# Loads of the last tokens' values without a common key, and small transfers of a recurrent step fewer and spread out

## The chip, the cores and the metric

The kernel runs on one core of one Trainium2 chip. Time is the device time in microseconds (us) of one execution, given as the median of several.

The names used below are PE (TensorE, matmul), ACT (ScalarE), DVE (VectorE), POOL (GpSimd) and SP (SyncE; here it computes nothing and only issues DMAs). "SPq" is SP's sequencer. "ring" is a set of SBUF buffers through which weights are streamed.

## The reference, cut to what matters

Two branches are mixed by a gate. Branch A is recurrent: 64 segments of 32 tokens, each with 8 memory rows in front of it. The first 8 output rows of a segment are the memory of the next.

```python
for s in range(n_seg):                               # 64 segments
    xs = x[:, s * seg_len:(s + 1) * seg_len, :]
    h = jnp.concatenate([mem, xs], axis=1)           # 8 + 32 rows of 1024
    q, k, v = (jnp.einsum('btd,dhe->bhte', h, W) for W in (Wq, Wk, Wv))   # shortened; 32 heads of 128
    ...                                              # masked softmax attention
    o = jnp.einsum('bhte,hed->btd', o, Wo)
    mem = o[:, :M, :]
    outs.append(o[:, M:, :])
b = gelu(x @ w_gate) * (x @ w_up) @ w_down           # branch B, an FFN, 1024 to 3584 to 1024
return g * a + (1 - g) * b
```

Wq, Wk, Wv and Wo are 8 MB each in bf16, 32 MB together, and every segment needs all of them. SBUF holds only a part, so the rest is read from HBM again in each of the 64 steps.

## The kernel before: the parts that matter

The weights are 64 pieces of 512 KB. 43 stay in SBUF. 21 are streamed in every step through a ring of five buffers. SP issues all transfers of a step in program order. The q, k, v of the last 8 tokens of a segment ("rest") don't depend on the memory, so they are computed once at the start and loaded in small parts (`vB`, `qkr`). The memory rows attend to these tokens too, so a step needs them; but their own output is not needed for the next memory, and its projection is done after the loop.

A helper records every operation with the regions that it reads and writes, and works out the waits. The line to keep in mind is the one for writes: a DMA that writes a region waits for the region's last writer.

```python
def _touch(self, op, reg, write, async_):
    # ... (cut) a region is a set of SBUF cells, or a key such as ("D", "v", 3)
    for k in keys:
        w, rd = c                                  # last writer, readers since
        if write:
            if w is not None and (w.sem is not None or w.eng != op.eng or async_):
                deps.append(w)                     # a DMA waits for the writer before it
            # ... and for the readers

def load_str():                                    # the next streamed piece, into the ring
    n = nst[0]; nst[0] += 1
    p, t = seq[n], ring[n % NRING]
    op("sp", lambda e: e.dma_start(dst(t, p), src(p)), wr=[t.r()], lane=f"ring{n % NRING}")

def load_v(s):                                     # values of the last 8 tokens: 4 groups x 8 partitions
    for g in range(4):
        op("sp", lambda e, g=g: e.dma_start(vB[32 * g:32 * g + 8, :, :]..., v_scr[g, NB * s:NB * s + NB, :]),
           rd=[("D", "v", NB * s // RB)], wr=[vB.r()], lane=f"vb{g}")

def start_step():                                  # runs at piece 2 of a step
    put_rest(s)                                    # four POOL copies out of qkr
    for f in pend: f()                             # the stores of the step before
    pend.clear()
    if not last:
        load_h(s + 1)
        load_qk(s + 1)

on(55, lambda: attend(1))                          # the last reader of vB in a step
on(56, lambda: load_v(s + 1) if not last else None)
for p in range(64):
    for f in at.get(p, ()): f()
    proj(p, s)                                     # matmuls of piece p; then load_str() if p is streamed

def store(s=s):
    for g in range(4):
        op("sp", lambda e, g=g: e.dma_start(a_scr[s, 0:NR, g * 256:(g + 1) * 256], a_bf[32 * g:32 * g + NR, :]), ...)
    op("sp", lambda e: e.dma_start(o_scr[:, s, :], orr...), ...)
pend.append(store)

def load_a(T):                                     # in the FFN: branch A's result for 128 tokens
    op("sp", lambda e: e.dma_start(asb[T % 2][:, :], a_scr[4 * T:4 * T + 4].rearrange("s t f -> (s t) f")), ...)
```

## Time and profile before

| | before |
|---|---|
| median time | 3469.65 us |
| a recurrent step | 39.0 us, 64 of them |
| DMA share, rate in the loop | 0.84, 294 GB/s |
| PE clock granted in the loop | 0.81 |
| FFN, from its first matmul to the end | 613.1 us |

The length of a step is the distance of the DVE writes of the next memory into `hT`: the first starts at 316.6 us, the 63rd at 2735.4 us, and there are 62 steps between them.

The page shows the span in 40 equal slices, one digit each, in tenths. PE and DMA are busy shares, PEclk is the granted PE clock.

```profile
span 3479.6 us, 84141 instructions
PE   6685666776677676777667667776776679999998
PEclk9897787888788877877878887888788889999999
DMA  7658878887888888888888888888888761514414
```

Slices 4 to 31, counted from 0, are the loop. Neither PE nor the DMA engines are full there. That calls for a closer look at one step. The windows view gives, for a stretch of time, the busy time of each engine, then the PE clock, the mean share of the 16 DMA engines and their rate. The share is the summed time of the packets over the time of 16 engines; it can pass 1, because packet records of one engine can overlap. The first line is the loop, the others are one step's end.

```profile
core 0: us, PE busy (x) PEld busy (x) DVE busy (x) ACT busy (x) POOL busy (x), PEclk, DMA share, GB/s
316.60:2735.40 2418.80, 1692.67 (x33604) 694.31 (x33604) 406.07 (x1303) 427.29 (x1116) 97.53 (x310) 0.81 0.84 294
...
1093.00:1095.00 2.00, 1.70 (x56) 1.21 (x52) 0.56 (x2) 0.50 (x2) 1.19 (x4) 1.00 1.08 405
1097.00:1099.00 2.00, 1.72 (x18) 0.69 (x22) 0.19 (x1) 0.00 (x0) 0.00 (x0) 0.66 0.17 62
1099.00:1101.50 2.50, 2.33 (x24) 0.68 (x16) 0.00 (x0) 0.41 (x1) 0.00 (x0) 0.59 0.05 13
1101.50:1106.00 4.50, 0.64 (x8) 0.29 (x12) 0.00 (x0) 0.19 (x1) 0.00 (x0) 0.83 0.67 214
```

The DMA engines go from full to almost nothing at 1097 us. PE still has some pieces then, and after 1101.5 us it has hardly any (0.64 us busy of 4.5). The timeline of SP in order of time tells why (start, length, line, destination and source, count).

```profile
1092.63 0.34 SPq L340 DMA_DIRECT2D ring_80<-in_A_Wk_dram  x1
1093.02 8.80 SPq L554 DMA_DIRECT2D vB<-v_scr  x4
1101.86 0.36 SPq L340 DMA_DIRECT2D ring_81<-in_A_Wq_dram  x1
...
1103.21 1.74 SPq L788 DMA_DIRECT2D a_scr<-a_bf  x4
1104.99 0.35 SPq L790 DMA_DIRECT2D o_scr<-orr  x1
1105.38 0.43 SPq L545 DMA_DIRECT2D hT_55<-xq_scr  x1
1105.86 0.46 SPq L549 DMA_DIRECT2D qkr<-qk_scr  x1
1106.36 0.50 SPq L340 DMA_DIRECT2D ring_79<-in_A_Wk_dram  x1
```

The four vB loads take 8.80 us of SP. The waits view (engine, line, what it waited for: us in total, times, longest) shows what it was waiting for over the whole loop.

```profile
SPq L340 <- PE pb L701: 868.0, 683, 4.4
SPq L554 <- DMA vB<-v_scr: 472.1, 189, 7.3
```

The first line is harmless in itself: SP waits until PE has freed a ring buffer. The second is a wait of one DMA for another; 189 is three waits in each of 63 steps.

### The profile page before, as it was taken

Reading aid. Unit: us, or ns where it says so; the run is one execution under the profiler, and the core shown is the slowest. Engines: PE = TensorE matmul, PEld = TensorE weight load, DVE = VectorE, ACT = ScalarE, POOL = GpSimd, SP = SyncE. Lnnn points to the kernel's source line nnn. Section 1 sums busy time; section 2 is a strip of 40 time slices with the busy share of each in tenths; the row PEclk is TensorE's granted clock in tenths of the full one; section 3 lists DMA queues with packets and bytes.
Section 4 is the critical chain, followed back from the end, with each engine's and each line's share of the span. In section 5 each row is a group of like instructions: output and inputs, shape, how many; then the busy total and the mean of one; then the engine's idle time right before and its main releaser. Section 6 shows DMA issues by size and latency. Waiting matters only on the chain.

```text
span 3479.6 us, 84141 instructions
## 1 busy us (share of the span) xinstructions
PE 2584.2 (74%) x38522; PEld 1095.3 (31%) x38566; DVE 758.9 (22%) x1837; ACT 631.1 (18%) x1453; POOL 143.5 (4%) x383
## 2 busy tenths in 40 slices
PE   6685666776677676777667667776776679999998
PEld 3332222332223222223222222232222234444443
DVE  1311111111111111111111111111111106344353
ACT  1111111111112111111111111111111113122121
POOL 2200000000000000000000000000000000000000
PEclk9897787888788877877878887888788889999999
DMA  7658878887888888888888888888888761514414
GB/s 238 181 140 297 288 277 296 305 307 268 292 301 306 286 290 294 296 292 278 290 297 296 293 283 300 301 312 282 302 290 311 278 237 52 206 66 140 151 61 151
DMA packets 440962, 881.35 MB, mean 253 GB/s; under 512 B 131736, under 2 KB 166552, under 8 KB 440096
## 3 DMA queue, kind: packets, MB, share of 16 engines
q1 hardware_dynamic: 362960, 849.49, 69.5%
q10 hardware_dynamic: 77648, 26.48, 3.2%
q8 instruction: 302, 4.95, 0.6%
q14 instruction: 52, 0.43, 0.0%
HBM read 846.48 MB, written 29.36 MB: 252 GB/s over the span
## 4 chain that ended last, share of the span: by engine, by line
DMA 47%; PE 42%; SPq 6%; issue 3%; DVE 2%; ACTq 1%; ACT 0%
PE pb L701 13%; DMA vB<-v_scr 12%; PE pb L919 11%; PE pb L953 4%; PE pb L712 3%; DMA ring_82<-in_A_Wk_dram 3%; PE pb L486 3%; DMA ring_82<-in_A_Wo_dram 2%; DMA ring_79<-in_A_Wo_dram 2%; DMA ring_80<-in_A_Wo_dram 2%; DMA ring_80<-in_A_Wk_dram 2%; DMA ring_78<-in_A_Wo_dram 2%; SPq L788 2%; DMA ring_81<-in_A_Wo_dram 2%; DMA ring_79<-in_A_Wk_dram 2%
## 5 line engine op out<-in xcount | busy, mean ns | idle before, releaser
L568 ACT ACTIVATE tok_76<-pb 128x512 bf16<-128x512 f32 x128 | 76.4, 597 | 615.1 <-PE pb L701 615.1
L568 ACT ACTIVATE tok_77<-pb 128x512 bf16<-128x512 f32 (+1 forms) x128 | 62.8, 490 | 545.9 <-PE pb L701 545.9
L571 DVE COPY kT_69<-pb 128x512 bf16<-128x512 bf16 x64 | 27.2, 424 | 574.3 <-PE pb L585 574.3
L927 ACT ACTIVATE s_162<-pb 128x512 f32<-128x512 f32 x112 | 66.8, 596 | 326.9 <-DVE osb_164 L968 172.5
L770 POOL COPY orr<-oT 128x256 bf16<-128x256 bf16 x64 | 25.6, 400 | 2383.0 <-DVE oT L571 2383.0
L571 DVE COPY qT_65<-pb 128x512 bf16<-128x512 bf16 x64 | 27.2, 424 | 438.2 <-PE pb L585 438.2
L571 DVE CAST oT<-pb 128x160 bf16<-128x160 f32 x256 | 71.1, 319 | 217.2 <-PE pb L682 217.2
L568 ACT ACTIVATE oT<-pb 128x160 bf16<-128x160 f32 x256 | 63.8, 301 | 248.6 <-PE pb L682 248.6
L701 PE MATMUL pb<-ring_78,hT_56 128*32 128x512 bf16 x384 | 47.7, 486 | 62.1 <-DMA ring_78<-in_A_Wq_dram 43.1
L701 PE MATMUL pb<-ring_78,hT_55 128*32 128x512 bf16 x384 | 47.1, 479 | 59.5 <-DMA ring_78<-in_A_Wk_dram 30.5
L701 PE MATMUL pb<-ring_82,hT_56 128*32 128x512 bf16 x384 | 46.9, 477 | 57.3 <-DMA ring_82<-in_A_Wq_dram 37.4
L701 PE MATMUL pb<-ring_81,hT_56 128*32 128x512 bf16 x384 | 45.2, 459 | 59.0 <-DMA ring_81<-in_A_Wq_dram 40.2
L701 PE MATMUL pb<-ring_79,hT_56 128*32 128x512 bf16 x384 | 46.8, 475 | 53.9 <-DMA ring_79<-in_A_Wq_dram 34.3
L701 PE MATMUL pb<-ring_80,hT_56 128*32 128x512 bf16 x384 | 45.5, 462 | 55.2 <-DMA ring_80<-in_A_Wq_dram 35.1
L701 PE MATMUL pb<-ring_80,hT_55 128*32 128x512 bf16 x384 | 47.6, 484 | 47.4 <-DMA ring_80<-in_A_Wq_dram 25.6
L701 PE MATMUL pb<-ring_82,hT_55 128*32 128x512 bf16 x384 | 47.4, 482 | 44.3 <-DMA ring_82<-in_A_Wq_dram 23.8
L701 PE MATMUL pb<-ring_81,hT_55 128*32 128x512 bf16 x384 | 47.4, 481 | 43.1 <-DMA ring_81<-in_A_Wq_dram 26.0
L701 PE MATMUL pb<-ring_79,hT_55 128*32 128x512 bf16 x384 | 47.4, 482 | 42.4 <-DMA ring_79<-in_A_Wq_dram 25.6
L611 DVE TENSOR_REDUCE nm_58<-pb 128x8 f32<-128x320 f32 x64 | 31.5, 492 | 197.6 <-PE pb L607 197.6
L953 PE MATMUL pb<-wd_141,GT 128*128 128x512 bf16 x299 | 70.0, 386 | 5.3 <-DMA wd_141<-in_B_w_down_dram 5.0
L953 PE MATMUL pb<-wd_140,GT 128*128 128x512 bf16 x294 | 67.9, 379 | 3.0 <-DMA wd_140<-in_B_w_down_dram 2.4
L568 ACT ACTIVATE kT_70<-pb 128x512 bf16<-128x512 bf16 x64 | 38.2, 597 | 175.3 <-PE pb L585 175.3
(482 smaller groups left out, 5186.5 us busy)
## 6 DMA issues: line engine op xcount, KB each, us to landing
ring_82<-in_A_Wq_dram SPq DMA_DIRECT2D x80, 512.0 KB, 7.2
ring_80<-in_A_Wq_dram SPq DMA_DIRECT2D x78, 512.0 KB, 7.2
ring_81<-in_A_Wq_dram SPq DMA_DIRECT2D x78, 512.0 KB, 7.4
ring_78<-in_A_Wo_dram SPq DMA_DIRECT2D x78, 512.0 KB, 6.8
ring_79<-in_A_Wo_dram SPq DMA_DIRECT2D x78, 512.0 KB, 6.7
ring_80<-in_A_Wo_dram SPq DMA_DIRECT2D x78, 512.0 KB, 6.6
ring_81<-in_A_Wo_dram SPq DMA_DIRECT2D x78, 512.0 KB, 6.7
ring_78<-in_A_Wq_dram SPq DMA_DIRECT2D x78, 512.0 KB, 7.2
```

What stands on the lines that cost most here:

```text
L486: ins = e.matmul(PB[b][:, 0:NRT], lhsT=w8[kc][:, c:c + 128], rhs=xrT[:, kc, :], start=(kc == 0), stop=(kc == KC - 1))
L568: op("act", lambda e: e.activation(o, i, ACTF.Copy), rd=rd, wr=wr)
L571: op("dve", lambda e: e.tensor_copy(o, i), rd=rd, wr=wr)
L611: op("dve", lambda e: e.tensor_reduce(nm[u][:, :, :].rearrange("p a b -> p (a b)"), PB[SS][:, 0:320].rearrange("p (a c) -> p a c", c=LQ), ...
L701: ins = e.matmul(PB[bk][32 * g:32 * g + 32, :], lhsT=h[:, kc, :], rhs=w[:, g * 512:(g + 1) * 512], start=(kc == 0), stop=(kc == KC - 1))
L712: ins = e.matmul(PB[A0][32 * g:32 * g + 32, 0:256], lhsT=oT[:, u, gp, 2 * jj + hh, 0:32], rhs=w[:, c:c + 256], start=(p == 48 and hh == 0) ...
L770: op("pool", lambda e: e.tensor_copy(orr[:, :, :, :].rearrange("p u x c -> p (u x) c"), oT[:, :, :, :, 32:40].rearrange("p u g j c -> p (u ...
L788: op("sp", lambda e, g=g: e.dma_start(a_scr[s, 0:NR, g * 256:(g + 1) * 256], a_bf[32 * g:32 * g + NR, :]), rd=[a_bf.r()], wr=[("D", "a", s ...
L919: ins = e.matmul(PB[bk][:, 0:FB], lhsT=w[:, kc, cc:cc + 128], rhs=xT[:, :, :, kc, :].rearrange("p t i c -> p (t i) c"), start=(kc == 0), s ...
L927: op("act", lambda e, hg=hg: e.activation(s1[:, :], hg, ACTF.Square, scale=SQ), rd=[BK(bg)], wr=[s1.r()])
L953: ins = e.matmul(PB[bank[2 * k + hf]][:, :], lhsT=GT[:, j, tb * 128:(tb + 1) * 128], rhs=w[:, jj, hf * 512:(hf + 1) * 512], start=(j == 0) ...
```

## The change

It has three parts. (1) Each vB group gets its own key, so that the four loads no longer wait for each other. (2) The four stores of `a_bf` become one, into a raw layout; the price is that the FFN has to collect a block of 128 tokens by eight DMAs instead of one. (3) The loads of h and qk for the next step move from piece 2 to pieces 5 and 8. The diff, cut to its core (the FFN's small buffers are also placed by a new allocator, which is cut here):

```diff
+        op("pool", lambda e: e.memset(nm[0][:, 0:1, 0:1], 0.0), rd=[vB.r()], wr=[("D", "vB", g) for g in range(4)])
 ...
-                   rd=[("D", "v", NB * s // RB)], wr=[vB.r()], lane=f"vb{g}")
+                   rd=[("D", "v", NB * s // RB)], wr=[("D", "vB", g)], lane=f"vb{g}")
 ...
-            op("pe", f, rd=[vA[u].r(), vB.r(), EE[u].r()], wr=[BK(b) for b in bo])
+            op("pe", f, rd=[vA[u].r(), EE[u].r()] + [("D", "vB", g) for g in range(4)], wr=[BK(b) for b in bo])
 ...
-                if not last:
-                    load_h(s + 1)
-                    load_qk(s + 1)
             on(2, start_step)
+            on(5, lambda: load_h(s + 1) if not last else None)
+            on(8, lambda: load_qk(s + 1) if not last else None)
 ...
-                for g in range(4):
-                    op("sp", lambda e, g=g: e.dma_start(a_scr[s, 0:NR, g * 256:(g + 1) * 256], a_bf[32 * g:32 * g + NR, :]),
-                       rd=[a_bf.r()], wr=[("D", "a", s // 4, "m", s, g)], lane=f"st{g}")
+                op("sp", lambda e: e.dma_start(a_raw[s, :, :], a_bf[:, :]), rd=[a_bf.r()], wr=[("D", "a", s)], lane="st")
 ...
-            op("sp", lambda e: e.dma_start(asb[T % 2][:, :], a_scr[4 * T:4 * T + 4].rearrange("s t f -> (s t) f")), ...)
+            for i in range(4):
+                for key, lo, hi, ap in (("m", 0, NR, a_raw[4 * T + i].rearrange("(g r) c -> r g c", g=4)[0:NR]),
+                                        ("r", NR, SEG, a_rest[32 * T + 8 * i:32 * T + 8 * i + 8].rearrange("r (g c) -> r g c", g=4))):
+                    op("sp", lambda e, lo=lo, hi=hi, ap=ap, i=i: e.dma_start(
+                        t[32 * i + lo:32 * i + hi, :].rearrange("r (g c) -> r g c", g=4), ap), ...)
```

More of the change, by code (lines that the diff above doesn't have):

```diff
@@ L246, in bass_gated_mix__memory_aug_recurrent_mem_tr__geglu_ffn__prompt_kernel @@
         o_scr = nc.dram_tensor("o_scr", [128, NSEG, 256], BF16)
-        a_scr = nc.dram_tensor("a_scr", [NSEG, SEG, D], BF16)
+        a_raw = nc.dram_tensor("a_raw", [NSEG, 128, 256], BF16)
+        a_rest = nc.dram_tensor("a_rest", [NRT, D], BF16)
         PB = [es.enter_context(nc.psum_tensor(f"pb{i}", [128, 512], FP32)) for i in range(8)]
@@ L814, in bass_gated_mix__memory_aug_recurrent_mem_tr__geglu_ffn__prompt_kernel, with al2 @@
         orT = [orT0, al("orT1", [128, SB, 256], at=low)]
-        cur[0] = low + 8192
         arb = [al(f"arb{i}", [128, D], at=wd[0].off + 4096 + 2048 * i) for i in range(2)]
         orX = [al("orX0", [128, 32, SB, NB], at=wg[3].off), al("orX1", [128, 32, SB, NB], at=wd[1].off)]
-        asb = [al(f"asb{t}", [128, D]) for t in range(2)]
-        tp = [al(f"tp{t}", [128, FB], FP32) for t in range(2)]
-        s1 = al("s1", [128, FB], FP32)
-        osb = [al(f"osb{t}", [128, D]) for t in range(2)]
-        dsb = [al(f"dsb{t}", [128, 512], FP32) for t in range(2)]
-        assert cur[0] <= res0
+        free = [(low + 8192, res0), (cur[0], top), (0, low if ring[0].off < low else 0)]
+        def al2(name, shape, dt=BF16):
+            nb = shape[1] * (4 if dt == FP32 else 2)
+            for k, (lo, hi) in enumerate(free):
+                if lo + nb <= min(hi, 16384 if lo < 16384 else hi):
+                    free[k] = (lo + nb, hi)
+                    return al(name, shape, dt, at=lo)
+            raise AssertionError(name)
+        asb = [al2(f"asb{t}", [128, D]) for t in range(2)]
+        tp = [al2(f"tp{t}", [128, FB], FP32) for t in range(2)]
+        s1 = al2("s1", [128, FB], FP32)
+        osb = [al2(f"osb{t}", [128, D]) for t in range(2)]
+        dsb = [al2(f"dsb{t}", [128, 512], FP32) for t in range(2)]
         def load_or(b):
@@ L893, in bass_gated_mix__memory_aug_recurrent_mem_tr__geglu_ffn__prompt_kernel @@
             dve_copy(ab[0:RB, 512:1024], PB[bs[1]][0:RB, :], [BK(bs[1])], [ab.r(512, 1024)])
-            op("act", lambda e, b=b, ab=ab: e.dma_start(a_scr[SB * b:SB * b + SB, NR:SEG, :],
-                                                       ab[0:RB, :]),
+            op("act", lambda e, b=b, ab=ab: e.dma_start(a_rest[RB * b:RB * b + RB, :], ab[0:RB, :]),
                rd=[ab.r()], wr=[("D", "ar", T) for T in range(SB * b // 4, (SB * b + SB) // 4)], lane=f"ar{b % 2}")
@@ L906, in load_a @@
         def load_a(T):
-            op("sp", lambda e: e.dma_start(asb[T % 2][:, :], a_scr[4 * T:4 * T + 4].rearrange("s t f -> (s t) f")),
-               rd=[("D", "a", T, "m", s, g) for s in range(4 * T, 4 * T + 4) for g in range(4)] + [("D", "ar", T)],
-               wr=[asb[T % 2].r()], lane=f"al{T % 2}")
+            t = asb[T % 2]
+            for i in range(4):
+                for key, lo, hi, ap in (("m", 0, NR, a_raw[4 * T + i].rearrange("(g r) c -> r g c", g=4)[0:NR]),
+                                        ("r", NR, SEG, a_rest[32 * T + 8 * i:32 * T + 8 * i + 8].rearrange("r (g c) -> r g c", g=4))):
+                    op("sp", lambda e, lo=lo, hi=hi, ap=ap, i=i: e.dma_start(
+                        t[32 * i + lo:32 * i + hi, :].rearrange("r (g c) -> r g c", g=4), ap),
+                       rd=[("D", "a", 4 * T + i) if key == "m" else ("D", "ar", T)], wr=[("D", "asb", T % 2, i, key)],
+                       lane=f"al{T % 2}{i}{key}")
         for fb in range(NFB):
@@ L966, in bass_gated_mix__memory_aug_recurrent_mem_tr__geglu_ffn__prompt_kernel @@
                             out=d[:, :], in0=asb[T % 2][:, cs], in1=PB[b][:, :], op=ALU.subtract),
-                           rd=[BK(b), asb[T % 2].r()], wr=[d.r()])
+                           rd=[BK(b)] + [("D", "asb", T % 2, i, k) for i in range(4) for k in "mr"], wr=[d.r()])
                         op("dve", lambda e, T=T, b=b, cs=cs, ob=ob, d=d: e.scalar_tensor_tensor(
```

## The prediction

> **What bounds it now.** The program has a start (to about 265 us), 64 recurrent steps (to about 2776 us), a pass over the last tokens, and the FFN. A step takes 39.0 us (distance of the DVE writes into hT). In the windows view the loop keeps the DMA engines 0.84 busy at 294 GB/s and PE about 0.70: neither is full. A step streams 21 weight pieces of 512 KB through 5 ring buffers, issued by SP in program order. The waits view for SP shows the hole: L554 (values of the last tokens, vB) waits for earlier vB loads, 472 us in total. All four write one recorded region, so each waits for the one before: first about 5.5 us (it queues behind ring pieces), then 1.5 and 1.5 us with nothing else queued. Behind them come three ring loads, four stores of a_bf (1.7 us of issue), o, h and qk. At 1097 to 1101.5 us the DMA share is 0.17 and 0.05. About 6.5 us of DMA time a step is idle, nearly all there. PE runs dry about 9.2 us a step on ring DMAs, and its clock after the gap is 0.5 to 0.6.
>
> **What changes.** (1) One key per vB group: four issues, about 1.1 us of SP, no wait; ring loads follow. (2) One a_bf store for four: 1.3 us less issue, 16 KB more. (3) The h and qk loads move three and six pieces later; qk waits for four POOL copies of 0.29 us, which at its old place would now stall SP. (4) Cost: an asb load becomes 8 DMAs of 512 B rows; SP issues 16 instead of 2 ahead of the w_down loads, twice per FFN block.
>
> **How much is critical.** Steps: packets add up to 32.8 us per step of 16 engines (about 29 at their median durations), the new floor. PE's own chain is 39.0 - 9.2 = 29.8 us, part of it at half clock, and should shorten. Both are close, so overlap won't be perfect: 33.0 us a step, an estimate. Gain 6.0 x 63.5 = 380 us.
> FFN: 14 more issues at 0.23 to 0.4 us, 3 to 5 us per pair. w_down is issued right after asb (2993.05, then 2993.43 us), and its landing (6.7 us) already ends a PE wait in the chain. I expect 3 us at each of 8 places, 25 us lost. The rest stays.
>
> 3470 - 380 + 25, about **3115 us**, range 3030 to 3220. Faster by over 2%: 0.97; within 2%: 0.02; slower: 0.01.
>
> The Trainium skill agrees on two points: "DMA: Bandwidth & Descriptors", Rules for kernel authors, says transfers under 64 KB pay mostly overhead (here a lone 16 KB vB load takes 1.5 us); "TensorE: Matmul & The Clock Gate", Part 1, says idling halves the clock (here 0.5 to 0.6 after the gap).
>
> **What would show it.** Steps of 32 to 34 us; SP's wait on vB gone from the waits, vB gone from the chain; DMA share in the loop 0.95 or more at about 340 GB/s; no slices near 0.05 at a step's end; loop clock up from 0.81; SP waiting for PE (L701, L712) to free ring buffers. In the FFN: longer PE waits on w_down, about 25 us in all.
>
> **What would make it wrong.** Five buffers too few to carry DMA over the step's end, so that DMA idles waiting for PE: 34 to 35 us a step. Packets that stretch when the queue is always full: share rises, GB/s doesn't. Or the reverse: median packets and a warmer PE give 30 to 31 us, about 3000. The FFN loss could be larger if 512 B rows on few engines block the w_down loads behind them.

## The result, and the profile after

| | before | after |
|---|---|---|
| median time | 3469.65 us | 2994.8 us |
| ratio, 95% interval | | 0.8637 [0.8606, 0.8668] |
| a recurrent step | 39.01 us | 31.18 us |
| DMA share, rate in the loop | 0.84, 294 GB/s | 1.01, 368 GB/s |
| PE clock in the loop | 0.81 | 0.95 |
| FFN | 613.1 us | 632.8 us |

A ratio here is the mean time of one kernel's runs over the mean of the other's of the same rounds, so it is not quite the ratio of the medians. Executions over 1.5% slower than the fastest of the same kernel are left out of the means.

The change is faster by 13.6%. The direction and the mechanism were predicted. The time was not: 2994.8 us lies below the range of 3030 to 3220 us.

The page of the changed kernel, the same lines as before:

```profile
span 2990.3 us, 84293 instructions
PE   5687777777777777777777777787776999989998
PEclk9888999999999999999999999899998999999999
DMA  8666999999999999999999999999999415060705
```

In the loop the DMA digits are now all 9, and the PE clock is 9 in all of its slices but one. The windows view of the loop and of one step's end:

```profile
310.40:2243.60 1933.20, 1485.29 (x33604) 650.19 (x33604) 405.86 (x1303) 429.68 (x1116) 97.51 (x310) 0.95 1.01 368
...
1023.00:1025.00 2.00, 1.86 (x77) 1.16 (x74) 0.56 (x2) 0.50 (x2) 0.62 (x2) 1.00 1.05 397
1025.00:1027.00 2.00, 1.35 (x36) 0.71 (x32) 0.00 (x0) 0.00 (x0) 0.95 (x4) 1.00 1.05 387
1027.00:1029.00 2.00, 1.06 (x18) 0.55 (x22) 0.48 (x2) 0.28 (x1) 0.00 (x0) 1.00 1.00 316
```

And the timeline of SP over the same place of a step:

```profile
1023.31 0.34 SPq L341 DMA_DIRECT2D ring_78<-in_A_Wk_dram  x1
1023.70 1.34 SPq L556 DMA_DIRECT2D vB<-v_scr  x4
1025.08 0.36 SPq L341 DMA_DIRECT2D ring_79<-in_A_Wq_dram  x1
...
1027.63 0.33 SPq L788 DMA_DIRECT2D a_raw<-a_bf  x1
1028.00 0.43 SPq L789 DMA_DIRECT2D o_scr<-orr  x1
1029.32 0.33 SPq L341 DMA_DIRECT2D ring_82<-in_A_Wk_dram  x1
1029.70 0.43 SPq L547 DMA_DIRECT2D hT_56<-xq_scr  x1
1030.17 0.47 SPq L341 DMA_DIRECT2D ring_78<-in_A_Wk_dram  x1
1030.69 0.55 SPq L551 DMA_DIRECT2D qkr<-qk_scr  x1
```

The vB loads take 1.34 us instead of 8.80 us, the wait on vB is gone from the waits view, and the small transfers stand between ring loads instead of in one block.

Where the 489.3 us between the two profiled spans (3479.6 and 2990.3 us) come from: 62 steps at 7.83 us each are 485.6 us; the start is 6.2 us shorter; from the last write of `hT` to the FFN it is 17.2 us shorter (131.1 to 113.9 us; the last step lies in it); the FFN is 19.7 us longer.

The prediction had a step fall to 33.0 us, because the packets of a step summed to 32.8 us of 16 engines, and it called that sum the new floor. The step went below it. The sum itself fell: 0.84 x 39.01 is 32.8 us, and 1.01 x 31.18 is 31.5 us. By the packet records of the trace between the first and the last write of `hT`, the mean packet of 4096 bytes (pieces of Wq, Wk, Wv) took 184.8 ns before and 174.3 ns after, with the same number of them and a median of 159 ns in both. So the question for the experiments was: what had stretched the packets before, and which part of the change took it away?

### The profile page after: what moved, and what is told of

Read it like the earlier page. It is cut to its first block, busy times and chain, and to the rows that moved or that the text cites. A ratio compares the mean times of both kernels' runs of the same rounds, so it can differ in the third digit from the quotient of the medians.

```text
span 2990.3 us, 84293 instructions
## 1 busy us (share of the span) xinstructions
PE 2381.1 (80%) x38566; PEld 1052.3 (35%) x38566; DVE 758.7 (25%) x1837; ACT 633.6 (21%) x1453; POOL 143.6 (5%) x384
## 4 chain that ended last, share of the span: by engine, by line
DMA 50%; PE 42%; issue 3%; SPq 2%; DVE 2%; ACT 1%; ACTq 1%; DVEq 0%
PE pb L929 12%; PE pb L703 9%; DMA ring_78<-in_A_Wq_dram 5%; DMA ring_81<-in_A_Wq_dram 5%; DMA ring_82<-in_A_Wq_dram 5%; PE pb L963 4%; DMA ring_79<-in_A_Wq_dram 4%; PE pb L714 4%; DMA ring_80<-in_A_Wq_dram 4%; DMA ring_80<-in_A_Wo_dram 3%; PE pb L488 3%; DMA ring_82<-in_A_Wo_dram 3%; DMA ring_81<-in_A_Wo_dram 3%; DMA ring_80<-in_A_Wv_dram 2%; DMA ring_78<-in_A_Wo_dram 2%
## 5 line engine op out<-in xcount | busy, mean ns | idle before, releaser
L963 PE MATMUL pb<-wd_141,GT 128*128 128x512 bf16 x304 | 73.2, 397 | 7.8 <-DMA wd_141<-in_B_w_down_dram 7.8
L573 DVE CAST a_bf<-pb 128x128 bf16<-128x128 f32 x64 | 18.6, 291 | 233.6 <-ACT a_bf L570 233.6
L963 PE MATMUL pb<-wd_140,GT 128*128 128x512 bf16 x304 | 71.9, 392 | 5.4 <-DMA wd_140<-in_B_w_down_dram 5.4
L963 PE MATMUL pb<-wd_142,GT 128*128 128x512 bf16 x288 | 69.6, 398 | 6.1 <-DMA wd_142<-in_B_w_down_dram 6.1
L703 PE MATMUL pb<-ring_78,hT_55 128*32 128x512 bf16 x384 | 42.0, 417 | 39.7 <-DMA ring_78<-in_A_Wk_dram 17.2
L703 PE MATMUL pb<-ring_81,hT_56 128*32 128x512 bf16 x384 | 40.3, 406 | 31.9 <-DMA ring_81<-in_A_Wq_dram 16.3
L570 ACT ACTIVATE a_bf<-pb 128x128 bf16<-128x128 f32 x64 | 17.7, 277 | 217.5 <-PE pb L714 217.5
L929 PE MATMUL pb<-xT,wg_144 128*128 128x512 bf16 x224 | 56.2, 396 | 7.9 <-DVE GT L945 7.9
L703 PE MATMUL pb<-ring_82,hT_56 128*32 128x512 bf16 x384 | 39.6, 397 | 27.6 <-DMA ring_82<-in_A_Wq_dram 13.9
L703 PE MATMUL pb<-ring_82,hT_55 128*32 128x512 bf16 x384 | 40.0, 403 | 25.9 <-DMA ring_82<-in_A_Wq_dram 15.4
L573 DVE CAST tok_77<-pb 128x256 bf16<-128x256 f32 x64 | 27.1, 424 | 131.8 <-ACT tok_77 L570 131.8
L703 PE MATMUL pb<-ring_80,hT_55 128*32 128x512 bf16 x384 | 39.9, 401 | 25.7 <-DMA ring_80<-in_A_Wk_dram 12.3
```

The lines of the kernel that those rows point to most:

```text
L570: op("act", lambda e: e.activation(o, i, ACTF.Copy), rd=rd, wr=wr)
L573: op("dve", lambda e: e.tensor_copy(o, i), rd=rd, wr=wr)
L703: ins = e.matmul(PB[bk][32 * g:32 * g + 32, :], lhsT=h[:, kc, :], rhs=w[:, g * 512:(g + 1) * 512], start=(kc == 0), stop=(kc == KC - 1))
L929: ins = e.matmul(PB[bk][:, 0:FB], lhsT=w[:, kc, cc:cc + 128], rhs=xT[:, :, :, kc, :].rearrange("p t i c -> p (t i) c"), start=(kc == 0), s ...
L963: ins = e.matmul(PB[bank[2 * k + hf]][:, :], lhsT=GT[:, j, tb * 128:(tb + 1) * 128], rhs=w[:, jj, hf * 512:(hf + 1) * 512], start=(j == 0) ...
```

## The experiments

Two theories at first. **A**: the vB chain was the whole loss of the steps; after the gap the ring restarts in a burst, and that stretches packets. Part 1 alone then gives everything. **B**: the four stores and the bunched h and qk loads, also issued by SP in front of the ring loads, hold things up as well.

A step and a share below are those of the loop, read in the same way as above. The four first runs shared their rounds.

### Part 1 alone

```diff
 # the kernel before, with the three changed lines of the vB keys only
-    wr=[vB.r()], lane=f"vb{g}")
+    wr=[("D", "vB", g)], lane=f"vb{g}")
```

> The kernel before with part 1 alone (one key per vB group). Theory A (the vB chain is the whole loss of the steps): a step falls from 39.0 to 31.0 to 31.6 us, the packets of 4096 bytes shrink from 185 to about 174 ns as in the changed kernel, and with the old single asb load the FFN stays at 613 us, so the total is about 2975 us, a little below the changed kernel. Theory B (the four stores and the bunched h and qk loads at a step's start also hold SP up): a step of 32.5 us or more, packets near 180 ns, total 3050 us or more.

Measured: 3099.35 us, ratio 0.8916 [0.8877, 0.8956]; a step 33.08 us; packets of 4096 bytes 184.6 ns; FFN 614.3 us. Theory B. Part 1 takes 5.93 us off a step, and it lands on the number that the prediction gave for the whole change; for part 1 alone nobody had predicted it. The other 1.90 us come from parts 2 and 3. The windows view of its loop:

```profile
314.30:2365.50 2051.20, 1558.54 (x33604) 671.72 (x33604) 405.69 (x1302) 427.90 (x1116) 97.52 (x310) 0.90 0.99 347
```

The engines were "busy" 0.99 of the time, and yet they moved only 347 GB/s, against 368 at 1.01. What SP did at a step's end there:

```profile
1040.34 2.43 SPq L340 DMA_DIRECT2D ring<-in_A_Wq_dram  x3
1043.08 1.53 SPq L789 DMA_DIRECT2D a_scr<-a_bf  x4
1044.66 0.38 SPq L791 DMA_DIRECT2D o_scr<-orr  x1
1045.08 0.43 SPq L546 DMA_DIRECT2D hT<-xq_scr  x1
1045.56 0.43 SPq L550 DMA_DIRECT2D qkr<-qk_scr  x1
1046.03 1.05 SPq L340 DMA_DIRECT2D ring<-in_A_Wk_dram  x2
```

From 1042.77 to 1046.03 us no ring load is issued. That is 3.3 us, which seven small transfers fill.

### All but part 1

```diff
 # the changed kernel, with the three vB lines as before
-    wr=[("D", "vB", g)], lane=f"vb{g}")
+    wr=[vB.r()], lane=f"vb{g}")
```

> The changed kernel without part 1: vB loads wait for each other again, one store and the spread loads stay. Theory A: a step of 38 to 39 us, SP waiting over 400 us on vB, total 3420 to 3490 us. Theory B: the store and the spreading are worth 2 us a step or more by themselves, total 3350 us or less.

Measured: 3425.18 us, ratio 0.9862 [0.9824, 0.9900]; a step 38.07 us; SP waited 387.5 us on vB in the stretch from 320 to 2230 us. Parts 2 and 3 without part 1 give 0.94 us a step; with part 1 in place they give 1.90 us. Theory A's numbers hold for this run. The parts are not additive: as long as the vB gap is there, it hides half of what the others cost.

### All but part 2, and all but part 3

```diff
 # e3_stores4: the kernel with part 1 and part 3; stores and the asb load as before
 # e4_bunch: the changed kernel with h and qk loads back in start_step, at piece 2
+                if not last:
+                    load_h(s + 1)
+                    load_qk(s + 1)
```

> The changed kernel without part 2: four stores a step and the single asb load of before, with the keys and the spread loads. Theory A: the steps stay at 31.2 us and the FFN gets its 20 us back (613 instead of 633 us): about 2970 us. Theory B: the three extra stores cost 1.3 us of SP a step and DMA idles for it: a step of 32 us or more, 3020 us or more.

> The changed kernel without part 3: h and qk loads back at the second piece of a step. Theory A: ring loads already queued hide SP's wait for the four POOL copies (about 1.2 us), step 31.2 to 31.6 us, total 2990 to 3020 us. Theory B: SP stands for 1.2 us or more with the ring empty, step 32 us or more, total 3045 us or more.

Measured: without part 2, 3029.06 us and a step of 31.73 us; without part 3, 3030.99 us and a step of 31.54 us. The first step lies between the two theories' numbers, its total in theory B's; the second step is still in theory A's range, its total between the two. In the profiles either part alone takes most of the 1.90 us (1.35 and 1.54 us), and together they add only a little. These profiles are the fastest of four executions each, 13 and 17 us under the medians, up to 0.2 and 0.3 us a step, so how little the second part adds is not sure. The pattern would fit one block of SP time that is made short enough: 3.3 us hurt, half of it hardly does. It was still only a pattern. So the next question was what in that block hurts: that SP is held up (**H**), or that the small packets get in the way of the ring's packets (**P**).

### The same small transfers, issued by ACT

```diff
 # the kernel with part 1 alone (e1_keys); a_scr stores, o_scr store, h and qk loads:
-    op("sp", lambda e: e.dma_start(...
+    op("act", lambda e: e.dma_start(...
```

> The kernel before with part 1 alone (33.1 us a step), and its four stores of a_bf, the store of o and the loads of h and qk issued by ACT instead of SP; the same DMAs at the same places of the program. Theory H (in the run of part 1 alone, SP is held up for 3.5 us at a step's start and refills the ring late): with SP free the step falls to 31.0 to 31.6 us, the total to 2960 to 3000 us. Theory P (the small packets slow the packets of the ring whenever they run together, whoever issues them): the step stays at 32.7 us or more, the packets of 4096 bytes stay at 183 ns or more, and the total at 3080 us or more.

Measured: 2977.18 us, ratio 0.8589 [0.8560, 0.8618]; a step 31.26 us; packets of 4096 bytes 174.2 ns; FFN 612.7 us. Theory H, in all three numbers. The same seven DMAs with the same packets at the same places of the program cost 1.8 us a step more from SP than from ACT. Its loop:

```profile
311.30:2249.30 1938.00, 1499.87 (x33604) 657.87 (x33604) 405.70 (x1302) 430.24 (x1116) 97.52 (x310) 0.95 1.01 367
```

### A hold-up without traffic, and its control

The last run moved traffic and hold-up together. This pair adds a hold-up with next to no bytes to the changed kernel.

```diff
+            def tiny():
+                for i in range(8):
+                    op("sp", lambda e, i=i: e.dma_start(d_scr[i, :, :], ident[0:1, 0:32]), ..., lane=f"dm{i}")   # control: "act"
+            on(2, tiny)
```

> The changed kernel with eight tiny stores (64 bytes each, one row) issued by SP at the third piece of every step, right after the stores of a step: about 8 x 0.3 us = 2.4 us in which SP issues nothing to the ring, and next to no bytes. Theory R (a ring refilled late is what stretches packets and opens gaps): the step rises from 31.2 to 32.5 us or more, the mean 4096-byte packet from 174 to over 180 ns. Theory T (it was the traffic of the small transfers itself that slowed the ring): with no traffic added, the step stays within 0.5 us of 31.2 us and the packets at 174 ns.

> The control of the run before: the same eight tiny stores at the same place, issued by ACT. Under both theories the step stays at 31.0 to 31.8 us and the packets at about 174 ns, unless ACT, held up for about 4 us, delays its first copy of the step, which is due at the ninth piece.

Measured: by SP, 3112.01 us, ratio 0.8994 [0.8958, 0.9031], a step of 32.84 us and packets of 179.6 ns (just under the 180 expected). By ACT, 2993.51 us, ratio 0.8644 [0.8610, 0.8678], a step of 31.10 us and packets of 173.7 ns. The loop of the first, then of the control:

```profile
314.30:2350.30 2036.00, 1537.64 (x33604) 656.83 (x33604) 406.18 (x1302) 428.00 (x1116) 97.51 (x310) 0.91 0.99 350
```

```profile
311.90:2240.10 1928.20, 1476.85 (x33604) 647.08 (x33604) 406.22 (x1303) 429.36 (x1116) 97.52 (x310) 0.96 1.01 369
```

In a step of the first run SP spent 2.34 us on the eight tiny stores (1043.30 to 1045.64 us). It cost 1.66 us a step against the changed kernel and 1.74 us against the control of the same rounds, longer packets and a lower PE clock, with no traffic to blame.

Two things can be added from the kept traces. First, how late the ring loads are: a load's issue minus the end of the last matmul on its buffer, summed over the 21 loads of a step. This is 36.1 us before, 4.6 us with part 1 alone, 3.2 and 2.3 us without part 2 and without part 3, 1.8 us in the changed kernel, 1.3 us with the small transfers by ACT, and 6.8 us against 2.0 us in this pair. With part 1 alone three loads in a row are 1.6, 1.2 and 0.5 us late in the median; by ACT each of these is 0.04 us late. (The sum does not rank the two slow runs, so it is not the whole measure.) Second, where the stretch is: of packets of 4096 bytes that start 4 to 6 us after a write of `hT`, just behind the hold-up, the mean is 249 ns with part 1 alone and 232 ns with tiny stores by SP, against 184 ns in the changed kernel, 189 ns with the small transfers by ACT and 180 ns in the control.

One rival is weakened but not excluded. By SP the small transfers go into the ring's own DMA queue (q1 in the DMA view), by ACT into another (q10), so both pairs change the queue along with the engine. In q1 the tiny packets are too little work to matter by themselves: eight of 11 ns a step, and eight more of 9 ns that come with them. The late issue itself is measured.

So a ring that is refilled late goes with stretched packets of the ring itself, with next to no added bytes, and it is SP's hold-up that makes it late. That is shown, up to the change of queue. How the DMA engines come to take longer over a packet then is not: the trace tells a packet's start and length, not what it waited for.

### Is it the bytes now? Half of the streamed Wo pieces

```diff
+            if p >= 48:    # wrong result on purpose: the second head of a streamed Wo piece is stale
+                op("sp", lambda e: e.dma_start(dst(t, p)[:, 0:1, :], src(p)[:, 0:1, :]), ...)
```

> The changed kernel, but of each streamed piece of Wo only the first of its two heads is loaded (wrong result on purpose): 6 x 256 KB = 1.57 MB less of 11.48 MB a step, the same instructions elsewhere. Theory DMA (the steps of the changed kernel are bound by DMA bytes): a step falls by about 13%, from 31.2 to 27.0 to 28 us, until PE's own chain (31.2 - 5.1 us of waits on ring loads = 26.1 us) binds. Theory PE (PE's chain of softmax and projections binds now): the step stays above 30 us.

Measured in one round of two executions: 2893.67 us (2883.95 and 2903.38); a step 29.66 us; DMA share 0.95, 334 GB/s. It hit neither theory. A step of the changed kernel does depend on bytes, but only 1.5 us of the expected 3.2 to 4.2 us came. The share fell, so the engines idled: averaged over the steps, the share was about 0.66 to 0.81 from eight to four us before a step's end, where the Wo pieces are used and PE is busy over 0.9. The saving was in one place, and five buffers do not carry it to another. A step is bound by bytes in its first part and close to bound by PE in its last. (The comparison with the reference does not see an error of this size in branch A, so it is no proof of this kind of correctness.)

### One ring buffer fewer, one resident piece more

```diff
-    NRING = 5
+    NRING = 4      # the freed 4 KB per partition hold a 44th resident piece; wo_t gets two more places in GT
```

> The changed kernel with four ring buffers instead of five; the freed 4 KB per partition hold one more resident piece, so 20 pieces are streamed a step instead of 21 (10.96 instead of 11.48 MB). Theory DMA with queue to spare: 31.2 x 10.96 / 11.48 = 29.8 us a step, total about 2905 us. If five buffers were needed to keep the DMA engines full: share falls below 0.97 and the step stays at 30.5 us or more, total 2950 us or more.

Measured: 3141.38 us, ratio 0.9066 [0.9041, 0.9091]; a step 33.49 us with 10.95 MB, against 31.18 us with 11.48 MB; share 0.95; packets of 4096 bytes 186.4 ns. Fewer bytes, slower steps, longer packets. This is a second way to the same effect, and not by late issue: measured as above, the loads are 1.4 us late in a step. But a load is issued 5.8 us ahead of its first use in the mean, against 6.5 us with five buffers. With less of the ring under way, packets stretch and gaps open. The fifth buffer was worth more than the piece it displaced.

### The FFN: who issues the eight loads

```diff
 # the changed kernel, load_a issued by ACT
-                    op("sp", lambda e, lo=lo, hi=hi, ap=ap, i=i: e.dma_start(
+                    op("act", lambda e, lo=lo, hi=hi, ap=ap, i=i: e.dma_start(
```

> The changed kernel with the eight asb loads of a token block issued by ACT instead of SP, so the w_down loads no longer stand behind them. If the FFN's 20 us come from SP's issue order: the FFN falls from 633 to about 605 to 613 us, PE's wait on w_down from 19 to 10 us or less, total about 2970 us. If they come from the 512-byte rows crowding the DMA engines: no change, 2990 to 3000 us.

Measured: 2992.76 us, ratio 0.8611 [0.8575, 0.8647]; no difference from the changed kernel that these runs could show (the median counts the slow execution, the ratio doesn't). The FFN took 620.2 us, between the two numbers that the theories named, and PE waited 17.1 us in it on w_down, not the 10 us or less expected of the issue order. It is read together with the next run.

### A combination meant to beat both

Keys, spread loads, the old four stores and the old single asb load, and every small transfer of a step and the asb load issued by ACT.

```diff
 # the kernel before, plus parts 1 and 3, plus
-    op("sp", ...)      # load_h, load_qk, the stores of a_bf and o, load_a
+    op("act", ...)
```

> A combination meant to beat both: the keys; h and qk loads and all step stores (the old four) issued by ACT, with the loads spread as in the change; the old single asb load, issued by ACT ahead of nothing that SP sends. Steps as with SP free (31.0 to 31.4 us), FFN 605 to 613 us with under 10 us of waits on w_down: total 2955 to 2980 us.

Measured: 2973.71 us (2964.99 to 2984.93), ratio 0.8581 [0.8556, 0.8607]; a step 31.11 us; FFN 607.6 us. It beats the kernel before clearly. Against the changed kernel the two were not timed in the same rounds; the control with ACT's tiny stores, which has the changed kernel's steps and its FFN code, took 2993.51 us in the rounds of this run. The profiled spans of the two are 18.8 us apart: 11.5 us of it are in the FFN (619.1 against 607.6 us), 11.4 us between the last write of `hT` and the FFN, and the start and the loop take some 4 us back. The waits of PE on w_down there, for the kernel before, the changed kernel, eight loads by ACT, and the combination (one load by ACT):

```profile
PE pb L953 <- DMA wd_141<-in_B_w_down_dram: 5.0, 4, 2.8
PE pb L953 <- DMA wd_140<-in_B_w_down_dram: 2.4, 4, 1.6
PE pb L953 <- DMA wd_142<-in_B_w_down_dram: 2.3, 1, 2.3
```

```profile
PE pb L963 <- DMA wd_141<-in_B_w_down_dram: 7.8, 3, 3.7
PE pb L963 <- DMA wd_142<-in_B_w_down_dram: 6.1, 2, 3.6
PE pb L963 <- DMA wd_140<-in_B_w_down_dram: 5.4, 2, 3.0
```

```profile
PE pb L963 <- DMA wd<-in_B_w_down_dram: 17.1, 15, 1.8
```

```profile
PE pb L953 <- DMA wd<-in_B_w_down_dram: 5.9, 8, 1.1
```

One load: 9.7 us from SP (10.6 to 11.0 in three other runs), 5.9 from ACT. Eight loads: 19.3 us from SP, 17.1 from ACT. So the eight loads cost some 10 us of these waits whoever issues them, and the issuing engine matters for 2 to 5 us.

### Ten half buffers

```diff
 # the combination, with
-        ring = [al(f"ring{i}", [128, 2048]) for i in range(NRING)]
+        ring = [al(f"ring{i}", [128, 1024]) for i in range(2 * NRING)]      # a half piece each, freed after its own matmuls
```

> The combination before, with ten ring buffers of 256 KB instead of five of 512 KB: the same bytes and space, each half piece freed and refilled as soon as its own matmuls are done. If late refill is what remains between the packets' sum at their median durations (about 29 to 30 us) and 31.2 us: a step of 30.0 to 30.7 us, total about 2920 us. If rows of 2 KB instead of 4 KB cost more than that (84 ns for 2048 bytes against 159 ns for 4096, 1.1 us a step), or SP with 42 issues a step becomes the limit: 31.3 us or more.

Measured: 3018.32 us, ratio 0.8711 [0.8682, 0.8740]; a step 32.02 us; share 1.02, but only 358 GB/s. PE waited less on the ring (3.74 us a step, against 4.52 us in the combination), so refill was better; the bytes were dearer. A packet of 2048 bytes took 91.1 ns in the mean (median 84), two of them 182 ns, against 173.6 ns for one of 4096 in the combination. So row length decided, the first of the two reasons in the second half of the expectation. The other, SP's 42 issues a step, did not bind: from 320 to 2230 us SP still waited 697.9 us for PE at the first line of the waits view alone.

### The steps of the runs side by side

| run | step, us | DMA share | GB/s | mean packet of 4096 bytes, ns |
|---|---|---|---|---|
| before | 39.01 | 0.84 | 294 | 184.8 |
| all but part 1 | 38.07 | 0.85 | 301 | 178.2 |
| part 1 alone | 33.08 | 0.99 | 347 | 184.6 |
| part 1 alone, small transfers by ACT | 31.26 | 1.01 | 367 | 174.2 |
| all but part 2 | 31.73 | 1.00 | 361 | 175.9 |
| all but part 3 | 31.54 | 1.01 | 364 | 177.4 |
| after | 31.18 | 1.01 | 368 | 174.3 |
| after, tiny stores by SP | 32.84 | 0.99 | 350 | 179.6 |
| after, tiny stores by ACT | 31.10 | 1.01 | 369 | 173.7 |
| after, four ring buffers | 33.49 | 0.95 | 327 | 186.4 |
| combination | 31.11 | 1.01 | 368 | 173.6 |

## Why the prediction was wrong, point by point

- **The vB chain is the hole in the steps, and without it SP goes on.** Right. SP's 472 us of waits are gone; part 1 alone takes 5.93 us off a step, and the prediction's gain per step was 6.0 us. That these two agree is partly luck: the 6.0 us were meant for all three parts.
- **PE's clock.** Right. It rose from 0.81 to 0.95 in the loop. The Trainium skill ("TensorE: Matmul & The Clock Gate", Part 1) has an idle PE fall to half clock; in this trace the recorded clock is 1.0 or 0.5 in the loop, and in the 3.4 us before a fall PE was busy 0.29 of the time in the mean, before a rise 0.96 (the kernel before, 139 falls). Every run with a late ring has a lower clock as well (0.90 with part 1 alone, 0.91 with SP held up).
- **"packets add up to 32.8 us per step of 16 engines (about 29 at their median durations), the new floor."** This is the step that failed. The step measured 31.18 us. The sum of packet durations is not an amount of work. It contains stretch, and the stretch changes with how the ring is refilled: the sum stayed at 32.7 us with part 1 alone and fell to 31.5 us with the whole change. Nor is it a bound: even the changed kernel's sum is a little above its step, as packet records overlap.
- **Parts 2 and 3 in the steps.** The prediction gave them no gain in its sum ("1.3 us less issue" was stated and then not counted). With part 1 in place they are worth 1.90 us a step, 1.90 x 63.5 = 121 us, nearly all of the miss. With the packets' sum taken as the floor, a shorter issue by SP had nothing left to gain. In the runs it did.
- **FFN, 25 us lost.** The size was near, 19.7 us between these two profiles, but in good part by luck. PE's waits on w_down grew by 9.6 us, not by 25. And the FFN varied between profiles: 618.3 to 632.8 us in seven runs with eight loads from SP, 612.7 to 615.2 us in four with one load from SP. The clock records tell why: in the FFN the clock was 0.5 for 13.1 us before and for 37.6 us after, and for 9.5 us in the shortest of the seven. With half of that time taken off, an estimate, the four are 606 to 607 us and the seven 613 to 616 us. So the eight loads cost about 8 us, and the other 12 us are the clock of this execution. Of the cost of the loads, the stated cause, SP's issue in front of w_down, is the smaller part; the eight loads themselves cost most, which the prediction had named only as a danger.
- **The sum.** 3470 - 380 + 25 against 3470 less 475. Of the 133 us between the 356 us expected and the 489 us between the two profiles, 63.5 x (33.0 - 31.18) = 116 us are the step, 5 us the FFN, and the remaining 12 us the start and the stretch behind the loop, which were taken as unchanged.
- **"Or the reverse: median packets and a warmer PE give 30 to 31 us, about 3000."** This is near to what came, in its numbers; but it was left outside the range, and its reason is only half right: the medians did not change, the stretch above them did.

What stays open: why a packet takes longer when the ring is refilled late; whether the remaining stretch (the changed kernel still has 174.3 ns in the mean over a median of 159 ns) can be had without shorter rows or more SBUF; how much of a late ring's cost goes by longer packets and how much by PE at half clock; whether the small transfers' place in the ring's queue adds to SP's hold-up; and why the clock is at 0.5 for 9.5 us of the FFN in one execution and for 37.6 us in another.

## What to carry to other kernels

When one engine's queue feeds a stream of large loads, a block of small transfers in that queue can delay the refill, so try them on another engine's queue or scatter them singly between the large ones, and look for DMAs that wait for DMAs only because the bookkeeping gives them one region. A busy share of DMA packets near 1 does not mean that the bytes are at their limit: compare GB/s and mean packet duration, not the share alone. Before calling a sum of packet durations a floor, compare its mean with its median, since what lies above the median may go away.

## What the Trainium skill lacked or had wrong

- "DMA: Bandwidth & Descriptors", Issuing engines are not separate DMA queues, says that spreading DMAs over issuing engines only saves the sequencer's issue time, which is "usually small relative to the DMA itself". Here that issue time (3.3 us for seven small transfers) was worth 1.8 us of a 33.1 us step (part 1 alone against the same with these issued by ACT, which puts them in another DMA queue as well), 3099 against 2977 us in all. The page lacks that it counts when it stands in front of a ring's refill.
- The same page, Specifications, gives 512 bytes as the least transfer for line rate. By this kernel's packets that row is too low: the rate still rises above it, with a median of 27 ns for 512 bytes (19.0 bytes per ns and engine), 84 ns for 2048 (24.4), 159 ns for 4096 (25.8). Halving the rows from 4096 to 2048 bytes made a step 0.9 us longer (31.11 to 32.02 us).
- No page that was read for this says that packet durations depend on how far ahead a queue is filled. The mean packet of 4096 bytes took 174 ns with the ring refilled in time, 180 ns with SP held up for 2.3 us a step, 185 ns with part 1 alone and 186 ns with four ring buffers; the DMA share was 0.95 to 1.01 in these four, the rate 327 to 368 GB/s.
